# Attention without GpSimd, a planned tail of expert products, and six weight tiles converted early, in a fused attention and two-expert kernel

## Chip, cores and metric

One core of a Trainium2 chip runs the whole program. The metric is the device time of one execution in microseconds. TensorE (PE) multiplies, VectorE (DVE), ScalarE (ACT) and GpSimd (POOL) do the elementwise work, SyncE (SP) issues most transfers.

## What is computed

```python
scores = scale * q @ k.T                      # 4 batches x 8 heads, 576 x 576, head size 64
thresh = scores.max(-1) - tau
attn = softmax(where(scores >= thresh, scores, -1e9))
x = (attn @ v) as [2304 tokens, 512]
h = x @ w_in; g = max(h,0) + alpha*min(h,0); x = g @ w_out      # 512 -> 2048 -> 512
h = x @ w_in2; out = (h * sigmoid(h)) @ w_out2                  # 512 -> 2048 -> 512
```

All is float32. The experts' products are made from three single-pass products of a high and a low part (TERMS), so weights and activations are split into a high and a low half first.

## The kernel before

**Attention.** The 32 heads are worked in 16 pairs. A pair has 9 units: units 0 to 7 are 128 query rows of one of the two heads, unit 8 holds the last 64 rows of both. For each unit PE makes the scores (L333, two units at a time, eight products of 288 columns; unit 8 four products), DVE copies them out of PSUM and takes the row extreme (L347, "max"), ACT takes the exponential (L360), a small ACT instruction makes the threshold (L367), and DVE masks and sums (L373, "mask": two inputs from SBUF). PE transposes the masked rows (L408), ACT copies the transposes out (L123), PE multiplies with v (L442, L449). The reciprocal of the row sums (L382, DVE) is spread over 64 columns (L388, POOL), transposed by PE (L414), copied by ACT, and multiplied in as DVE takes the result out of PSUM (L456, L463) into X. The scores have two PSUM tiles of two banks (psS), transposes three banks, results one.

**Order.** Nothing is scheduled by the compiler inside attention: each operation is entered in a table with engine, assumed duration, priority and what it needs, and `plan` writes out one order for each engine from these durations. PE's order is fixed by the list CYCLE (Q score products, T transposes of the masked rows, R the bank with the last key block, Tr the transposes of the spread reciprocals, P the products with v, each with the pair it belongs to); the other engines take what is ready, by priority. PE changes its kind of product (`mode`) 11 times in a cycle of one pair.

**Weights.** `wconv` (L149 to L173) turns one 128 x 512 weight tile, loaded as 64-bit numbers into `wraw`, into its two halves: three ACT instructions, four on DVE (L159, L161, L163, L173) and two on POOL (L169, L171). Four of the first group's eight tiles are converted within attention, from unit WI = 60 on, one every WS = 12 units; the input split of the first 512 tokens (`xs0`, L548) follows from unit 104 on.

**Experts.** A job is a group of 512 hidden columns by a chunk of 512 tokens (the last 256): four blocks of hidden columns of 12 products each (`mm_h`, L202) into one of four PSUM banks, the activation on ACT and DVE (L211, L212 or L221, L222), its split (L123, L119), and, three blocks later, the products of `ymm` (L590, L599). The input split of later chunks is ACT and POOL work (L123, L119). These instructions are placed by the compiler's scheduler, which also merges them between those of attention. Their pools lie in the memory that attention's pools leave, and wait for the whole of these. The last products are added to ACC2 on DVE (L609) and stored by SP (L610).

Of the kernel before, what the change touches and what calls it, by code (L numbers as in the profile page):

```python
# [33 lines left out]
WI = 60  # L34
WU = 9
WS = 12
WN = 4
# [3 lines left out]
WT = 30  # L41
# [10 lines left out]
def mode(n):  # L52
    return {"pv": "v", "pv8": "v", "t": "t", "tr": "t"}.get(n[0], "t" if n[1] % 9 == 0 else "q")


def plan(ops, order, seq):
# [14 lines left out]
    def able(e):  # L71
        return [n for n in cand[e] if e != "PE" or n == seq[pe]]

    while any(able(e) for e in free):
# [3 lines left out]
        if e == "PE":  # L78
            pe += 1
            if mode(n) != last:  # L80
                t = max(t, free[e] + SWITCH)
            last = mode(n)
# [13 lines left out]
def attn_moe_moe(  # L96
# [52 lines left out]
    def wconv(stage, pool, wi, wo, g, j):  # L149
# [26 lines left out]
    def load_w(stage, pools, wi, wo, g, r0=()):  # L176
        r = list(r0)
        for j in range(len(r), NC + G):
            it = wconv(stage, pools[j // NC], wi, wo, g, j)
# [18 lines left out]
    def mm_h(ps, w, fl, xs, n):  # L198
        k = 0
        for c in range(NC):  # L200
# [31 lines left out]
    wA, xs0 = [], {}  # L232

    with ExitStack() as pa:
# [9 lines left out]
        psS = ent(name="psS", bufs=2, space=PSUM)  # L244
# [32 lines left out]
        warm = psT.tile([128, 512], F32, tag="t", name="t")  # L277
        for _ in range(WU):
            T.matmul(warm, zero[:, :128], zero, start=True, stop=True)
# [16 lines left out]
        def load(i):  # L296
            src = q_in[pairs[i]], k_in[pairs[i]]
            after = [qk(9 * (i - 2) + 1)] if i > 1 else []
# [3 lines left out]
            for x in (1, 0):  # L302
                def go(x=x):
                    nc.sync.dma_start(raw(i)[:, x, :QW[x]], src[x])
                op(("ld", i, x), "SP", 0.0 if i == 0 else 0.6, 1 if i else -4, after, go if i else lambda: None, 3.9 - 0.6 * x if i == 0 else 3.6)
            loadv(i, after, 2)

        def first(src):
# [3 lines left out]
            nc.sync.dma_start(raw(0)[:, 0, 512:], src[0][:, 512:])  # L312
            A.dma_start(sc[:, 0:1], tau[0:1].unsqueeze(0).to_broadcast([128, 1]))
            nc.sync.dma_start(raw(0)[h0, 0, :512], src[0][h0, :512])
            A.dma_start(raw(0)[h1, 0, :512], src[0][h1, :512])
# [68 lines left out]
        def spread(i, ch):  # L384
# [3 lines left out]
            P.tensor_copy(RS[i, ch][:, :n], stat(i)[:, 2, a:z].unsqueeze(2).to_broadcast([128, n, 64]))  # L388
# [285 lines left out]
```

## Time and profile before

| | |
|---|---|
| median of 3 runs | 1095.7 us (1095.08 to 1095.94) |
| the profiled execution: time / span | 1095.02 us / 1093.2 us |
| PE busy | 1077.0 us (99%) |
| DVE / ACT / POOL busy | 745.0 / 599.1 / 413.6 us |
| mean granted TensorE clock | 0.994 |
| first score product / last product with v / first product after it | 4.66 / 305.71 / 308.27 us |

Attention takes the first 307 us, the experts the rest. Because busy PE hides slow products, the table is read with rows that show starts of instructions: the distance between the same instruction in two pairs is the time of a pair.

### The profile page before, as it was taken

The numbers are of one execution on the slowest core, as the hardware profiler recorded it, in microseconds if no ns is written. First come the engines' busy times: TensorE is split into PE (matmuls) and PEld (weight loads), VectorE is DVE, ScalarE is ACT, GpSimd is POOL, SyncE is SP. The second block draws the span as 40 slices with busy tenths as digits, with TensorE's granted clock in tenths as the row PEclk, the third lists the DMA queues.
The fourth block names the chain that finished last, engine by engine and source line by source line (L and its number), as shares of the span: only waits on it lengthen the run. The fifth ranks groups of instructions, "written<-read, shape, count | busy, mean of one in ns | idle before, by whom it ended". The sixth has DMA issues, their size and how long they took to land.

```text
span 1093.2 us, 15460 instructions
## 1 busy us (share of the span) xinstructions
PE 1077.0 (99%) x5705; PEld 837.9 (77%) x5705; DVE 745.0 (68%) x1382; ACT 599.1 (55%) x1129; POOL 413.6 (38%) x339
## 2 busy tenths in 40 slices
PE   8999999999999999999999999999999999999998
PEld 5666656556767888888888888888888888888887
DVE  6989999989456677848755883764378568634343
ACT  5777878877555765535533553564555445334321
POOL 0100131320155566528525662662365346424210
PEclk8999999999999999999999999999999999999999
DMA  3212222211022222201110120121012002000112
GB/s 105 65 60 65 79 84 85 79 60 41 19 78 77 77 62 75 77 1 58 63 34 20 60 77 1 39 78 39 1 58 78 20 20 78 1 1 1 39 58 77
DMA packets 19259, 57.10 MB, mean 52 GB/s; under 512 B 2416, under 2 KB 2544, under 8 KB 19184
## 3 DMA queue, kind: packets, MB, share of 16 engines
q1 hardware_dynamic: 18880, 55.84, 15.8%
q8 instruction: 45, 0.74, 0.3%
q10 hardware_dynamic: 304, 0.28, 0.1%
q14 instruction: 30, 0.25, 0.1%
HBM read 51.39 MB, written 4.72 MB: 51 GB/s over the span
## 4 chain that ended last, share of the span: by engine, by line
PE 74%; DVE 6%; issue 3%; POOL 2%; ACT 2%; DMA 0%; DVEq 0%; POOLq 0%; ACTq 0%; SPq 0%
PE h L202 33%; PE y L599 18%; PE y L590 14%; PE s L333 3%; PE pv L442 3%; PE t L408 3%; DVE e L373 2%; POOL we L171 1%; DVE x L347 1%; DVE wa L161 1%; POOL wa L169 1%; DVE w L173 0%; ACT acc L228 0%; DVE wm L159 0%; DVE r L212 0%
## 5 line engine op out<-in xcount | busy, mean ns | idle before, releaser
L202 PE MATMUL h<-xs,w 128*128 128x512 f32 (+1 forms) x1920 | 431.1, 368 | 3.1 <-DVE r L212 3.1
L202 PEld LDWEIGHTS h<-xs,w 128*128 128x128 f32 x1920 | 337.8, 188 | 66.2 <-DVE r L212 4.9
L590 PE MATMUL y<-g,w 128*128 128x512 f32 (+1 forms) x960 | 215.0, 368 | 0.4 <-ACT acc L228 0.4
L599 PE MATMUL y<-w,g 128*128 128x512 f32 x864 | 213.7, 390 | 0.0
L590 PEld LDWEIGHTS y<-g,w 128*128 128x128 f32 x960 | 169.0, 188 | 31.6 <-ACT acc L228 0.7
L599 PEld LDWEIGHTS y<-w,g 128*128 128x128 f32 x864 | 160.7, 188 | 32.4
L119 DVE TENSOR_TENSOR g<-r,g 128x512 fp32r<-128x512 f32 (+1 forms) x160 | 140.7, 879 | 52.4 <-ACT g L123 51.1
L169 POOL TENSOR_TENSOR wa<-wa,w 128x512 f32<-128x512 f32 x64 | 84.0, 1313 | 207.3 <-ACT w L165 86.2
L119 POOL TENSOR_TENSOR xs<-acc,xs 128x512 fp32r<-128x512 f32 (+1 forms) x80 | 106.5, 1361 | 133.2 <-ACT xs L123 133.1
L123 ACT ACTIVATE g<-r 128x512 fp32r<-128x512 f32 (+1 forms) x160 | 94.0, 588 | 90.0 <-DVE r L222 46.6
L119 POOL TENSOR_TENSOR xs<-X,xs 128x512 fp32r<-128x512 f32 (+1 forms) x76 | 104.2, 1399 | 57.5 <-ACT xs L123 57.3
L347 DVE TENSOR_SCALAR_CACHE_REDUCE x<-s,nsc 128x576 f32<-128x576 f32 x144 | 112.4, 815 | 13.0 <-PE s L333 11.5
L360 ACT ACTIVATE e<-x,m 128x576 f32<-128x576 f32 x128 | 96.3, 781 | 43.5 <-DVE x L347 42.9
L373 DVE SCALAR_TENSOR_TENSOR e<-x,m,e 128x577 f32<-128x577 f32 x128 | 110.1, 881 | 8.1 <-ACT m L367 7.7
L222 DVE TENSOR_TENSOR r<-h,r 128x512 f32<-128x512 f32 (+1 forms) x80 | 50.7, 634 | 95.0 <-ACT r L221 94.9
L333 PE MATMUL s<-raw 64*128 64x288 f32 (+1 forms) x576 | 110.3, 437 | 5.1 <-DVE x L347 4.3
L388 POOL COPY rb<-m 128x256 f32<-128x256 f32 (+1 forms) x48 | 27.6, 576 | 211.8 <-PE t L414 100.3
L173 DVE TENSOR_TENSOR w<-we,wa 128x512 fp32r<-128x512 f32 x64 | 58.7, 918 | 61.1 <-POOL we L171 52.0
L221 ACT ACTIVATE r<-h 128x512 f32<-128x512 f32 (+1 forms) x80 | 43.8, 548 | 102.5 <-PE h L202 102.0
L171 POOL TENSOR_TENSOR we<-we,wm 128x512 f32<-128x512 f32 x64 | 93.6, 1462 | 13.7 <-ACT wm L167 13.1
L212 DVE SCALAR_TENSOR_TENSOR r<-r,neg,h 128x512 f32<-128x512 f32 (+1 forms) x80 | 55.0, 689 | 48.6 <-ACT r L211 48.4
L165 ACT ACTIVATE w<-wa 128x512 fp32r<-128x512 f32 x64 | 40.5, 633 | 82.2 <-DVE wa L161 75.4
(63 smaller groups left out, 1054.9 us busy)
## 6 DMA issues: line engine op xcount, KB each, us to landing
wraw<-in_w1i SPq DMA_DIRECT2D x16, 512.0 KB, 3.7
wraw<-in_w1o SPq DMA_DIRECT2D x16, 512.0 KB, 3.4
wraw<-in_w2i SPq DMA_DIRECT2D x16, 512.0 KB, 3.6
wraw<-in_w2o SPq DMA_DIRECT2D x16, 512.0 KB, 3.5
rv<-in_v SPq DMA_DIRECT2D x16, 480.0 KB, 3.4
raw<-in_q SPq DMA_DIRECT2D x15, 320.0 KB, 3.2
out<-o SPq DMA_DIRECT2D x18, 256.0 KB, 2.0
raw<-in_k SPq DMA_DIRECT2D x15, 288.0 KB, 2.8
```

The lines of the kernel that those rows point to most:

```text
L119: le.tensor_tensor(out=lo, in0=src, in1=hi.bitcast(F32), op=ALU.subtract)
L123: e.activation(out=dst, in_=src, func=AF.Copy)
L169: nc.gpsimd.tensor_tensor(out=a, in0=a, in1=w[:, 0].bitcast(F32), op=ALU.subtract)
L171: nc.gpsimd.tensor_tensor(out=e, in0=e, in1=m, op=ALU.mult)
L173: V.tensor_tensor(out=w[:, 1], in0=e, in1=a, op=ALU.add)
L202: nc.tensor.matmul(ps[:, :n], w[c][:, a, fl * 128:(fl + 1) * 128], xs[c][:, b, :n], start=k == 0, stop=k == 3 * NC - 1,)
L333: T.matmul(SP[u + k][:, hf, :S // 2], RAW[i][p, 0, q], RAW[i][p, 1, c], start=True, stop=True)
L347: V.tensor_scalar(out=x.rearrange("p (a b) -> p a b", a=2), in0=SP[u][:, :, :S // 2], scalar1=nsc, scalar2=None, op0=ALU.mult, op1=ALU.min ...
L360: A.activation(out=ES[u], in_=xts[u % XB][:, 1:S + 1], func=AF.Exp, bias=mcol(u, 0), scale=-1.0)
L373: V.scalar_tensor_tensor(out=e, in0=x, scalar=mcol(u, 1), in1=e, op0=ALU.is_le, op1=ALU.mult, accum_out=mcol(u, 2))
L590: nc.tensor.matmul(ys[e][:, :n], w[NC + fl][:, a, e * 128:(e + 1) * 128], gt[:, c, :n], start=fl == 0 and k == 0, stop=fl == G - 1 and k == 2,
L599: nc.tensor.matmul(ys[s], gt[:, a, s * 128:(s + 1) * 128], w[NC + fl][:, c, :], start=fl == 0 and k == 0, stop=fl == G - 1 and k == 2,)
```

## The change

- POOL leaves attention: the spread becomes an ACT instruction, and the two POOL instructions of `wconv` go to DVE there (the experts' later weights keep POOL).
- Six weight tiles instead of four are converted from unit 20 on, one every 14 units; the other two of the first group begin near the end of attention (unit 140). The split of the second chunk of tokens is also made in attention's table, on ACT and DVE.
- The units are worked as 0 to 8 instead of 8, 0 to 7, the CYCLE is another, with 9 changes of mode. The first pair's loads are cut otherwise, and the next pair's loads wait for the first score product.
- PE's order may take in fillers where `plan` sees PE idle: 32 products of zeros (z) at the start, and the 16 pieces (three products each) of the first job's hidden products (h), which now go into the two score tiles at the end of attention.
- The experts' pools wait tile by tile (`reuse_waits="tile"`); their four hidden banks are opened when the score tiles are given back.
- The last output tile is multiplied, added and stored in two column halves, the second stored by ACT's queue.

```diff
-WI = 60
+WI = 20
+WT = 4
-WS = 12
-WN = 4
+WF = 32
+WS = 14
+WN = 6
-    "T0:-1 T4:-1 Tr0:-1 Rr0:-1 Tr8:0 Rr8:0 Q4:0 Tr1:-1 P0:-1 "
-    "P8:0 Q6:0 P1:-1 P2:-1 Rr1:-1 T1:0 Q8:1 T2:0 T3:0 "
-    "T5:0 Q0:1 P3:-1 P4:-1 T6:0 T7:0 Q2:1 T8:1"
+    "Q2:-1 T6:-2 T2:-2 T7:-2 T0:-2 Tr1:-2 Q4:-1 T8:-2 Rr1:-2 "
+    "P0:-2 P1:-2 P2:-2 Q6:-1 T3:-1 T4:-1 T1:-1 Q8:-1 Tr8:-2 "
+    "T5:-1 Tr0:-1 Rr8:-2 Rr0:-1 Q0:0 P3:-2 P8:-2 P4:-2"
...
-        return [n for n in cand[e] if e != "PE" or n == seq[pe]]
+        c = cand[e]
+        if e == "PE":
+            fill = [n for n in c if n[0] in "hz"]
+            c = [n for n in c if n == seq[pe]]
+            if fill and (not c or ready[c[0]] > max(free[e], ready[fill[0]]) + ops[fill[0]][1]):
+                c = fill
+        return c
...
-        nc.gpsimd.tensor_tensor(out=a, in0=a, in1=w[:, 0].bitcast(F32), op=ALU.subtract)
-        nc.gpsimd.tensor_tensor(out=e, in0=e, in1=m, op=ALU.mult)
+        e2.tensor_tensor(out=a, in0=a, in1=w[:, 0].bitcast(F32), op=ALU.subtract)
+        e2.tensor_tensor(out=e, in0=e, in1=m, op=ALU.mult)
...
-        seq = [(i, t) for i in range(NP) for t in (8, 0, 1, 2, 3, 4, 5, 6, 7)]
+        seq = [(i, t) for i in range(NP) for t in range(9)]
...
-            P.tensor_copy(RS[i, ch][:, :n], stat(i)[:, 2, a:z].unsqueeze(2).to_broadcast([128, n, 64]))
+            A.activation(out=RS[i, ch][:, :n], in_=stat(i)[:, 2, a:z].unsqueeze(2).to_broadcast([128, n, 64]), func=AF.Copy)
...
-        for j in range(WN):
-            conv(j, [qk(WI + j * WS if j < NC else NU - WT)])
+        for j in range(NC + G):
+            conv(j, [qk(WI + j * WS if j < WN else NU - WT)])
...
+                need = [("h", f, c - 1)] if c else [("h", f - 1, NC - 1), ("max", NU - 2 + f // 2)]
+                op(("h", f, c), "PE", 0.68, 0, need + [("xl", 0, c), ("w", c, 9)], go, 0.9)
...
+        for k in range(WF):
+            op(("z", k), "PE", 0.22, 0, [("z", k - 1), ("ld8",)], idle)
...
-        ent = lambda **k: pb.enter_context(tc.tile_pool(**k))
+        ent = lambda **k: pb.enter_context(tc.tile_pool(reuse_waits="tile", **k))
...
+                    parts = 2 if g == NG - 1 and ti == NT // 128 - 1 else 1
+                    wd = DM // parts
...
+                            q = nc.scalar if x else nc.sync
+                            q.dma_start(out[ti * 128:(ti + 1) * 128, cs], o[:, cs])
```

## Rows read from the trace of the kernel before

**Rows 1.** The page, busy time, share of the span and instructions of PE.

```profile
PE 1077.0 (99%) x5705; PEld 837.9 (77%) x5705; DVE 745.0 (68%) x1382; ACT 599.1 (55%) x1129; POOL 413.6 (38%) x339
```

**Rows 2.** Windows: busy time (instructions) by engine, granted clock, DMA share, GB/s.

```profile
10.00:25.00 15.00, 15.00 (x81) 10.51 (x80) 12.59 (x37) 9.26 (x20) 1.33 (x3) 0.66 0.13 42
...
225.00:230.00 5.00, 5.00 (x34) 2.14 (x32) 4.41 (x11) 3.89 (x8) 0.00 (x0) 0.66 0.00 0
...
125.00:240.00 115.00, 109.79 (x750) 65.07 (x747) 109.25 (x282) 91.98 (x180) 29.19 (x30) 0.99 0.23 73
```

**Rows 3.** Timeline of PE, unit 8's scores of four pairs: start, duration, [idle before].

```profile
20.84 1.40 PE L333 MATMUL s<-raw 128*128 128x288 f32 x4
...
87.69 1.14 PE L333 MATMUL s<-raw 128*128 128x288 f32 x4
...
121.74 1.14 PE L333 MATMUL s<-raw 128*128 128x288 f32 x4
...
250.76 1.14 PE L333 MATMUL s<-raw 128*128 128x288 f32 x4
```

**Rows 4.** Timeline of PE from 36.3 to 40.5 us.

```profile
36.34 0.60 PE L408 MATMUL t<-ident,e 128*128 128x128 f32 x4
36.77 1.14 PE L333 MATMUL s<-raw 128*128 128x288 f32 x4
37.75 1.47 PE L408 MATMUL t<-ident,e 128*128 128x128 f32 x12
39.15 1.42 PE L333 MATMUL s<-raw 64*128 64x288 f32 x8
```

**Rows 5.** Timeline of DVE, POOL and PE: two maxes; a mask beside GpSimd.

```profile
119.68 0.82 DVE L347 TENSOR_SCALAR_CACHE_REDUCE x<-s,nsc 128x576 f32<-128x576 f32 x1
...
120.42 0.81 DVE L347 TENSOR_SCALAR_CACHE_REDUCE x<-s,nsc 128x576 f32<-128x576 f32 x1
...
139.28 1.78 POOL L171 TENSOR_TENSOR we<-we,wm 128x512 f32<-128x512 f32 x1
...
139.86 1.82 DVE L373 SCALAR_TENSOR_TENSOR e<-x,m,e 128x577 f32<-128x577 f32 x1
...
142.48 1.23 PE L333 MATMUL s<-raw 64*128 64x288 f32 x6 [0.59 <-DVE x L347]
```

**Rows 6.** Timeline of POOL, DVE and PE from 217 to 227 us.

```profile
217.40 5.88 POOL L119 TENSOR_TENSOR xs<-X,xs 128x512 fp32r<-128x512 f32 x4 [4.44 <-ACT xs L123]
...
222.09 1.81 DVE L373 SCALAR_TENSOR_TENSOR e<-x,m,e 128x577 f32<-128x577 f32 x1
...
224.70 2.34 PE L333 MATMUL s<-raw 64*128 64x288 f32 x8 [0.27 <-DVE x L347]
```

**Rows 7.** Timeline of DVE and PE, the first 12 us.

```profile
5.63 0.15 DVE L137 TENSOR_SCALAR ge<-sc 128x1 f32<-128x1 f32 x1 [4.22 <-DMA sc<-in_tau]
...
6.60 1.63 PE L333 MATMUL s<-raw 64*128 64x288 f32 x8 [0.80 <-DMA raw<-in_q]
...
9.59 2.27 PE L333 MATMUL s<-raw 64*128 64x288 f32 x8 [1.36 <-DVE x L347]
```

**Rows 8.** Timeline of ACT and PE after attention, and PE's waits in total.

```profile
306.84 1.09 ACT L211 ACTIVATE r<-h 128x512 f32<-128x512 f32 x2 [1.33 <-PE pv L442]
...
308.27 3.92 PE L202 MATMUL h<-xs,w 128*128 128x512 f32 x16 [1.53 <-DVE r L212]
...
PE h L202 <- DVE r L212: 3.1, 3, 1.5
```

**Rows 9.** Timeline of DVE: instructions of the conversion and of the input split.

```profile
125.06 0.41 DVE L159 TENSOR_SCALAR wm<-wm 128x512 int32<-128x512 int32 x1
...
225.31 1.88 DVE L548 TENSOR_TENSOR xs<-X,xs 128x512 fp32r<-128x512 f32 x3
```

**Rows 10.** Lines by form: ACT's smallest copy out of PSUM (count, busy us, mean ns).

```profile
L123 ACT ACTIVATE q<-t 128x256 f32<-128x256 f32 x16 | 6.3, 394 | 0.0
```

**Rows 11.** Timeline of DVE at the end of the program.

```profile
1088.89 1.29 DVE L609 TENSOR_TENSOR o<-y,X 128x512 f32<-128x512 f32 x2 [3.14 <-PE y L599]
```

More of the change, by code (lines that the diff above doesn't have):

```diff
@@ L196, in xsplit, with mm_h @@
         return xs
-    def mm_h(ps, w, fl, xs, n):
-        k = 0
-        for c in range(NC):
+    def mm_h(ps, w, fl, xs, n, cs=range(NC)):
+        k = 3 * cs[0]
+        for c in cs:
             for a, b in TERMS:
@@ L230, in accum @@
             V.tensor_tensor(out=dst, in0=ps, in1=dst, op=ALU.add)
-    wA, xs0 = [], {}
+    scores = ctx.enter_context(ExitStack())
+    psS = scores.enter_context(tc.tile_pool(name="psS", bufs=2, space=PSUM, side="right"))
+    wA, xs0, hs0 = [], [{}, {}], {}
     with ExitStack() as pa:
@@ L276, in attn_moe_moe, with idle @@
         ops = {}
-        warm = psT.tile([128, 512], F32, tag="t", name="t")
+        warm = psV.tile([128, 512], F32, tag="pv", name="pv")
+        def idle():
+            T.matmul(warm, zero[:, :128], zero, start=True, stop=True)
         for _ in range(WU):
-            T.matmul(warm, zero[:, :128], zero, start=True, stop=True)
+            idle()
         def op(name, eng, dur, prio, deps, fn, fin=None):
@@ L504, in attn_moe_moe @@
                 free = users(etiles[n][0], 2 * etiles[n][1]) if n >= 0 else []
-            op(("exp", u), "ACT", 0.667, 0, [("max", u)] + free, lambda u=u: expo(u), 0.82)
+            op(("exp", u), "ACT", 0.667, 2, [("max", u)] + free, lambda u=u: expo(u), 0.82)
             g = 0 if t == 8 else t // 2 + 1
@@ L513, in attn_moe_moe @@
                 op(("recip", i, ch), "DVE", 0.1, 0, us, lambda i=i, ch=ch: recip(i, ch), 0.25)
-                op(("spread", i, ch), "POOL", 0.4, 0, [("recip", i, ch), ("tr", bank.get(before.get((i, ch))))], lambda i=i, ch=ch: spread(i, ch), 0.6)
+                op(("spread", i, ch), "ACT", 0.18 if ch == 2 else 0.28, 1, [("recip", i, ch), ("tr", bank.get(before.get((i, ch))))], lambda i=i, ch=ch: spread(i, ch), 0.34 if ch == 2 else 0.44)
         order = {}
@@ L537, in attn_moe_moe @@
                 order["pv", i, kt] = ("pv", i, kt - 1)
[L538 to L548 removed]
+            op(("evac", i), "DVE", 0.62, -1, [("pv", i, KT - 1)], lambda i=i: evac(i), 0.78)
@@ new lines, in attn_moe_moe, with go @@
+        for f in range(G):
+            for c in range(NC):
+                def go(f=f, c=c):
+                    if f % 2 == 0 and c == 0:
+                        hs0[f] = psS.tile([128, 2, 512], F32, tag="s", name="s")
+                    mm_h(hs0[f - f % 2][:, f % 2], wA, f, [xs0[0][x] for x in range(NC)], 512, (c,))
+                need = [("h", f, c - 1)] if c else [("h", f - 1, NC - 1), ("max", NU - 2 + f // 2)]
+                op(("h", f, c), "PE", 0.68, 0, need + [("xl", 0, c), ("w", c, 9)], go, 0.9)
+                order["h", f, c] = need[0]
@@ L616, in attn_moe_moe @@
             oi = order.index((m, g))
-            if xs0:
-                xs = [xs0.pop(c) for c in range(NC)]
+            if (m, g) == (1, 0) and t0 < 1024:
+                xs = [xs0[t0 // 512][c] for c in range(NC)]
             else:
@@ L622, in attn_moe_moe @@
             for fl in range(G):
-                ps = psH.tile([128, 512], F32, tag="h", name="h")
-                mm_h(ps, w, fl, xs, n)
+                if (m, g, t0) == (1, 0, 0):
+                    ps = hs0[fl - fl % 2][:, fl % 2]
+                else:
+                    if psH is None:
+                        scores.close()
+                        psH = ent(name="psH", bufs=4, space=PSUM, side="right")
+                    ps = psH.tile([128, 512], F32, tag="h", name="h")
+                    mm_h(ps, w, fl, xs, n)
                 gt = (act1 if m == 1 else act2)(bt, bg, ps, g * G + fl, n, 512, nc.scalar, V)
```

91 lines of the change are left out of this document (48 added, 43 removed).

## The prediction

> **What bounds the kernel now.** I read the page first. PE is busy 99% of the span [rows 1], but a PE that waits inside a product or runs at half clock is busy too, so I looked at the distance between equal instructions. Unit 8's score products start at 87.69 and, two pairs later, at 121.74 [rows 3]: 17.02 us a pair. Is that PE's own work? Twelve transposes that start at 37.75 are followed at 39.15 by the next scores, and four that start at 36.34 by unit 8's at 36.77 [rows 4]: 0.108 for one transpose, no idle time between, and about 0.10 more where the kind of product changes (1.40 less 12 x 0.108). So in an undisturbed pair PE is the bound, with DVE close behind: two maxes start 0.74 apart [rows 5], and 18 of these and of the equally long masks make 13.3 us of the 17.
>
> Then I looked for pairs that take longer. From 121.74 to 250.76 lie seven pairs and 129.0 us [rows 3]; seven undisturbed ones take 119.2, so 9.8 us are lost there, in the stretch in which weights are converted. Rows 5 show the commonest kind: POOL's product for a weight runs from 139.28 for 1.78, the mask beside it takes 1.82 instead of 0.82, and the scores behind it wait until 142.48. The lost time is the mask's extra 1.0. The stretch has three of these, 3.0 us. The other 6.8 fall in one place: four POOL subtractions of a later chunk's split, merged into attention by the compiler, hold POOL for 5.88 from 217.40, a mask again takes 1.81, PE runs dry [rows 6], and the windows show a granted clock of 0.66 for 225 to 230, that is, part of it at 1.2 GHz instead of 2.4 [rows 2]. Eight products that start at 224.70 take 2.34.
>
> The start is the second place: unit 8's first scores are at 4.66 and the next pair's at 20.84 [rows 3], 16.2 us in which PE has only some 8 us of work at full clock (four pairs of scores at 1.35 by rows 4, unit 8 at 0.98, the rest about 1.6, my estimate). The granted clock for 10 to 25 is 0.66 and DVE is busy 12.59 of the 15 us [rows 2].
>
> The third is the border: after attention PE waits 1.53 for DVE and in all 3.1 us at three places [rows 8], the later two with the weights that were not converted in time, and 0.4 for an ACT copy. From there on, PE runs 785 us of expert products without gaps, and nothing in the change makes them fewer.
>
> **The change, part by part.**
>
> *Fewer changes of kind.* 9 instead of 11 a pair, 2 x 0.10 x 16 pairs: about -3.0. This counts in full only while PE is the bound.
>
> *POOL out of attention.* The collisions go, up to -9.8. What takes their place is DVE work. A weight tile cost DVE four instructions and now six: four with two inputs at 0.63 (1.88 for three, the end shared) and two at 0.41 [rows 9], 3.3 us. One tile every 14 units is 2.15 a pair, with 13.3 for maxes and masks and some 1.3 for outputs and reciprocals (estimate): 16.75 of a pair's 16.83. So DVE has hardly any slack from unit 20 to unit 104. These instructions come last by priority, and a late weight hurts nobody until unit 144, so they slide; but one that has begun holds back a max for up to 0.63, PE waits for the max, and two score tiles give little cover. Lower end: nothing is lost, since in the before too a pair with conversion work but no collision shows no loss. Upper end: each of 36 instructions holds PE for 0.3 on average, 11 us. I take 1.5, near the lower end, because the rows nearest to it (conversion work in undisturbed pairs) cost nothing: net -8.3.
>
> A rule of the Trainium skill speaks against this part: "VectorE: DVE Perf Modes", section "The DRAIN you can't avoid", says that an instruction cannot issue until the one before has emptied the pipe, and to keep the count of instructions low. In rows 5 the second max starts 0.74 after the first, which lasts 0.82: the trace has the two overlap. By the rule DVE would need more than PE in these pairs; its time stands with the rivals.
>
> *The spread on ACT.* POOL's work becomes three ACT instructions a pair of at most 256 columns. The nearest row is a copy of 256 out of PSUM, 0.39 [rows 10]; 3 x 0.39 is 1.2 a pair. ACT is busy 92 of 115 us in the conversion stretch [rows 2], 80%, and goes to 87%. It hides behind PE, if the queue is kept: the spread stands between exponentials, and behind it wait PE's Tr transposes and then P's last block. If that cover goes, a late Tr costs at most one exponential, about 0.7, a pair. I take zero, since the list puts Tr several products after the masks.
>
> *The start.* The fillers keep PE occupied where it waited 0.80 for q and 1.36 for a max [rows 7], and the next pair's loads no longer compete with the first q. The first max still waits for tau, which lands at 5.6 in both [rows 7]. DVE then needs 15 instructions of 0.74, 11.1 us, until about 21; it took 15. So at most 3.9 is to be had; at worst the fillers (32 x 0.22, 7 us) are in PE's way by about 1. I take -2.5, because half the stretch ran at half clock and the score products at 2.3 and more sit in the chain from score to max. What is late next is the masks.
>
> *The end of attention.* The first job's 48 hidden products already lie between the last pairs' products (the scheduler did it), so moving them into the list gains about nothing. Converted weights and the second chunk's split take away two of three waits, about 2.0 [rows 8]. The first wait I expect to stay: ACT's activation starts at 306.84, released by the last product with v [rows 8], because its tile lies in memory that attention's last tiles hold; waiting tile by tile helps only where the tile under it is free earlier. Here a hidden bank lies in a two-bank score tile, so the next job waits for two activations instead of one, up to +0.7. Together -1.7, with -3.5 and +0.7 as ends. DVE gets two tiles (6.6) and eight splits (5.0) here; in the tail there are hardly any maxes left, so it hides.
>
> *Transfers.* SP issues the weight loads earlier and waits at each for its one staging buffer; behind it stand the loads of the pair after next, needed more than a pair later, so nothing. Attention's ACT queue takes the same small number of loads at the start.
>
> *The last tile.* Two additions, 1.29 in all, end the kernel [rows 11]; with halves there are three, serial on DVE, the last one shorter, its store half the size. I take 0, with 0.3 either way.
>
> **Sum.** 3.0 + 8.3 + 2.5 + 1.7 = 15.5 off the profiled execution's 1095.0, so 1079.5. The profiled one stands 0.7 below the median of 1095.7; for the median I give 1080.
>
> **Rivals.**
>
> *DVE at its limit.* Conversion instructions hold maxes back by 0.3 each, without PE running dry: 11 instead of 1.5, so 1089.5. For it: 16.75 of 16.83. Against it: undisturbed conversion pairs at 17.02 before. 0.12.
>
> *Merged work comes back.* The change does not do what it says: with pools that wait tile by tile the compiler can place later splits or weights, POOL's among them, into attention's end, and the event of rows 6 happens once again there, 6.8: 1087. Against it: the second chunk's split is in the table now, and the third needs buffers that only the first job's products free. 0.10.
>
> *DVE starves PE (slower).* Where DVE falls behind for longer than PE's list can bridge, PE runs dry and its clock falls to 1.2 GHz as after 224. Each time costs the 6.8 of that place. With all six tiles, 41 us: about 1120. It decides from three such events on (15.5 / 6.8). For it: no slack on DVE. Against it: that event needed ACT, POOL and DVE late together. 0.05.
>
> *DVE issues at full durations.* 18 x 0.82, 1.6 for the rest and 2.3 for the conversion, with no overlap, make 18.7 a pair against 16.83, over nine pairs 17 us: 1097, no change within the error. That is what the skill's DRAIN section named above would give; rows 5 speak against it. 0.03.
>
> *More than I count.* The masks beside POOL's small copies get shorter too, the pair falls to 16.5 and the start and border give their upper ends: 1080 - 5 - 1.4 - 1.8, about 1072. 0.08.
>
> **Numbers.** The forecast has 0.62, its own range 1076 to 1084. For 8 in 10 the range must reach the first two rivals on one side and part of the last on the other: 1072.5 to 1090. A difference of 0.2%, 2.2 us, is what a measurement of this kernel can tell from none. Faster: forecast, first two rivals and the last, 0.92; same 0.03; slower 0.05.
>
> **What the new profile would show.** Right: 16.8 a pair for most pairs, no mask above 0.9 until the last pair, a granted clock of 1.00 for 10 to 25 and 225 to 230, POOL idle until the experts, the second pair's scores earlier by two or three us, no wait of the hidden products for weights. Wrong: PE's scores waiting for DVE in many pairs between units 20 and 104 (the limit), a POOL subtraction before the last product with v beside a long mask (merged work), a clock below 1.00 after 30 us (starving), or fillers that run while a max is ready.

## The result and the profile after

The changed kernel takes 1078.1 us (median of four runs, 1078.02 to 1078.86) against 1095.6 for the kernel before on the same chip: a ratio of 0.9842, interval [0.9825, 0.9859]. 1080.0 was forecast, 1072.5 to 1090. The profiled execution took 1078.86, its span 1077.1, so 16.1 of span are gone. The total fits; its parts do not, as the rest of this document shows.

The page of the changed kernel: busy time, share of the span and instructions of each engine.

```profile
PE 1067.9 (99%) x5749; PEld 835.3 (78%) x5749; DVE 745.3 (69%) x1403; ACT 606.3 (56%) x1177; POOL 357.4 (33%) x271
```

Beside [rows 1], POOL has lost 56 us of work and, but for short instructions in the first 6 us, is idle until 287 us; PE's 99% says as little as before. The windows of the changed kernel (columns as in [rows 2]):

```profile
10.00:25.00 15.00, 14.77 (x85) 8.50 (x84) 13.62 (x39) 10.62 (x21) 0.00 (x0) 1.00 0.16 45
125.00:240.00 115.00, 114.36 (x841) 70.99 (x840) 114.14 (x317) 101.14 (x214) 0.00 (x0) 1.00 0.26 79
225.00:230.00 5.00, 5.00 (x31) 2.58 (x29) 5.00 (x13) 5.00 (x11) 0.00 (x0) 1.00 0.03 10
295.00:305.00 10.00, 7.35 (x26) 5.56 (x25) 7.23 (x11) 4.63 (x8) 5.29 (x4) 0.83 0.17 52
```

The clock is full (2.4 GHz) where it was 0.66, at 10 to 25 and 225 to 230. DVE is busy 114.14 of 115 us in the conversion stretch, up from 109.25. And there is a new low clock, 0.83, at 295 to 305, which is the border (the passage from attention to the experts).

Now the pairs. The timeline of PE of the changed kernel: unit 8's scores of five pairs and, behind the first, the scores that follow; ahead of these the first scores of the third pair, and at the end those of the last:

```profile
36.28 1.24 PE L345 MATMUL s<-raw 64*128 64x288 f32 x8
...
99.81 1.14 PE L345 MATMUL s<-raw 128*128 128x288 f32 x4
...
101.97 1.24 PE L345 MATMUL s<-raw 64*128 64x288 f32 x8
103.14 1.08 PE L454 MATMUL pv<-pt,rv 128*64 128x512 f32 x4
...
132.62 1.14 PE L345 MATMUL s<-raw 128*128 128x288 f32 x4
...
198.24 1.14 PE L345 MATMUL s<-raw 128*128 128x288 f32 x4
...
216.35 1.14 PE L345 MATMUL s<-raw 128*128 128x288 f32 x4
...
249.37 1.14 PE L345 MATMUL s<-raw 128*128 128x288 f32 x4
...
251.53 1.24 PE L345 MATMUL s<-raw 64*128 64x288 f32 x8
```

A pair is now 16.41 us (99.81 to 132.62 are two), where it was 17.02 and 16.8 was forecast. From 132.62 to 249.37 seven pairs take 116.75; seven times 16.41 is 114.9, so 1.9 are lost instead of 9.8. Nearly all of that is one pair, 18.11 from 198.24.

**Where the 16.1 us are.** The last product with v starts at 305.71 in the kernel before and at 278.57 now, 27.1 earlier. In the kernel before, the 48 hidden products of the first job lay ahead of it in five groups, which took 11.6 by the distance of each to what follows it (285.19 to 289.41, 292.65 to 294.82, 295.61 to 296.85, 297.21 to 299.81, 300.39 to 301.71). Now they follow it in one row and take 11.0 (279.53 to 290.55). So attention itself is 15.6 shorter, and the hidden products 0.5. The last pair's first scores are, in the kernel before:

```profile
267.81 1.14 PE L333 MATMUL s<-raw 128*128 128x288 f32 x4
```

With it the 15.6 can be divided. The third pair begins at 36.28 instead of 36.77 [rows 4], so start and first two pairs gave 0.5. The last pair begins 16.3 earlier (251.53), so the 13 pairs between gave 15.8: 13 by 0.61 are 7.9, and the long pairs are the other 7.9 (9.8 - 1.9). The last pair and the tail behind it, without the hidden products, take 0.7 longer. From the last product with v to the last additions (1088.89 [rows 11] and 1072.73 now), the hidden products left out on both sides, lie 783.2 and 783.1: the border and all that follows gave nothing. The end after them is unchanged.

**A pair, from inside.** Why 0.61 a pair where two changes of kind at 0.10 were counted? The timeline of PE of the kernel before, the scores behind unit 8's of [rows 3]; under it a window of 0.02 us (90.30 to 90.32) of the same scores, and last such a window (102.05 to 102.07) of the changed kernel's:

```profile
90.07 1.57 PE L333 MATMUL s<-raw 64*128 64x288 f32 x8
91.57 1.08 PE L442 MATMUL pv<-pt,rv 128*64 128x512 f32 x4
...
90.07 0.51 PE L333 MATMUL s<-raw 64*128 64x288 f32 x1
...
101.97 0.51 PE L345 MATMUL s<-raw 64*128 64x288 f32 x2
```

And DVE's timeline in the kernel before, a mask and the readout that ends a max:

```profile
87.92 0.94 DVE L373 SCALAR_TENSOR_TENSOR e<-x,m,e 128x577 f32<-128x577 f32 x1
...
90.27 0.08 DVE L347 DVE_READ_ACCUMULATOR x<-s,nsc 128x1 f32 x1
```

The eight products are two units of four, one on each half of the array's rows, and run side by side: at 101.97 in the new kernel both start together (x2) and the group passes in 1.17 (to 103.14). At 90.07 in the kernel before one of them runs alone (x1 at 90.30); the other needs the score tile that the max gives back at 90.35, and the group takes 1.50 (to 91.57). That is 0.33, once a pair, and no view of idle time shows it, because PE is busy. What is left of the 0.61 is 0.28: the two changes of kind, 0.14 each by this subtraction.

The 0.33 may have two causes. The old list puts these scores close behind the max. But the mask at 87.92 also runs beside one of POOL's spread copies and takes 0.94 where its neighbours take 0.79 to 0.81, and DVE has no gap from there to that max. So up to 0.13 of the 0.33 can be POOL's copy, which the change took out as well; the runs below do not separate the two.

**The long pair.** The timeline of DVE, then of PE, of the changed kernel:

```profile
201.33 0.69 DVE L180 TENSOR_TENSOR w<-we,wa 128x512 fp32r<-128x512 f32 x1
201.94 0.68 DVE L565 TENSOR_TENSOR xs<-X,xs 128x512 fp32r<-128x512 f32 x1
202.54 0.81 DVE L359 TENSOR_SCALAR_CACHE_REDUCE x<-s,nsc 128x576 f32<-128x576 f32 x1
203.27 0.82 DVE L359 TENSOR_SCALAR_CACHE_REDUCE x<-s,nsc 128x576 f32<-128x576 f32 x1
...
209.12 1.23 PE L345 MATMUL s<-raw 64*128 64x288 f32 x6 [0.64 <-DVE x L359]
```

One product of the conversion and one of the split, back to back, put 1.21 us ahead of two maxes; another such two (198.65 and 199.25) lie 2.7 us before. DVE has no free time to make that up, and some units later scores wait. No long instruction and no low clock is involved; this is what is left of 9.8.

**The start.** PE, then DVE, of the changed kernel:

```profile
5.14 1.88 PE L345 MATMUL s<-raw 64*128 64x288 f32 x8
...
20.43 1.35 PE L345 MATMUL s<-raw 64*128 64x288 f32 x8
...
7.05 0.82 DVE L359 TENSOR_SCALAR_CACHE_REDUCE x<-s,nsc 128x576 f32<-128x576 f32 x1 [1.28 <-PE s L345]
```

The first scores are now two units' eight products instead of unit 8's four. They take 1.88 here, at a full clock, and the first max starts at 7.05, where it started at 6.11. The order of units alone does not explain that: in the ten runs below that begin with the same scores, they take 1.24 to 1.97 and the first max starts at 6.36 to 7.14. What stretches them was not found. The fillers keep the clock up, and from the first max to the second pair's first scores pass 13.4 us now (7.05 to 20.43) and 14.7 before (6.11 to 20.84 [rows 3]), where 11.1 were counted: between the maxes DVE still waits for the threshold that ACT makes (0.36, 0.37 and 0.27) and for unit 8's scores (0.59). So the second pair starts 0.4 earlier here, where 2.5 were forecast; in the nine other runs with the fillers its scores start at 19.53 to 20.49.

**The border.** PE, DVE, ACT and POOL of the changed kernel, after attention:

```profile
279.53 11.18 PE L209 MATMUL s<-xs,w 128*128 128x512 f32 x48
...
298.80 4.51 PE L625 MATMUL y<-g,w 128*128 128x512 f32 x12 [2.65 <-ACT g L130]
...
292.07 1.78 DVE L126 TENSOR_TENSOR g<-r,g 128x512 fp32r<-128x512 f32 x1
293.77 1.50 DVE L166 TENSOR_SCALAR wm<-wm 128x512 int32<-128x512 int32 x1
295.31 1.66 DVE L168 SCALAR_TENSOR_TENSOR wa<-wraw,wm 128x512 int32<-128x512 int32 x1
...
297.00 0.63 ACT L172 ACTIVATE w<-wa 128x512 fp32r<-128x512 f32 x1 [3.88 <-DVE wa L168]
...
290.30 6.12 POOL L126 TENSOR_TENSOR xs<-X,xs 128x512 fp32r<-128x512 f32 x4
```

The hidden products no longer wait for anything: the three waits of [rows 8], 3.1, are gone. In their place y waits once, 2.65, for the third hidden tile's ACT copy. Read the queues backwards: that copy stands in ACT's queue behind L172, which rounds a weight tile of the second group and waits 3.88 for DVE; DVE's instructions for it (L166, L168) take 1.50 and 1.66 instead of 0.43 and 0.68, as POOL does the subtractions of the third chunk's split beside them. The clock falls behind the wait: the next 12 products take 4.31 (the hidden products after them start at 303.11) where 12 take 2.72 at full clock (36 from 290.64 to 298.80 in a run below). 0.83 over 10 us is 3.4 us at 1.2 GHz, 1.7 lost. Three waits have turned into one, with other work ahead of it.

**The end.** The last additions of the changed kernel:

```profile
1072.73 1.35 DVE L646 TENSOR_TENSOR o<-y,X 128x512 f32<-128x512 f32 x3 [3.30 <-PE y L641]
```

Three additions take 1.35 where two took 1.29 [rows 11]. From there to the end of the span are 4.4 us, and 4.3 before.

### The profile page after: what moved, and what is told of

Read it like the earlier page. It is cut to its first block, busy times and chain, and to the rows that moved or that the text cites. A ratio compares the mean times of both kernels' runs of the same rounds, so it can differ in the third digit from the quotient of the medians.

```text
span 1077.1 us, 15422 instructions
## 1 busy us (share of the span) xinstructions
PE 1067.9 (99%) x5749; PEld 835.3 (78%) x5749; DVE 745.3 (69%) x1403; ACT 606.3 (56%) x1177; POOL 357.4 (33%) x271
## 4 chain that ended last, share of the span: by engine, by line
PE 94%; DVE 3%; ACT 1%; issue 1%; DMA 0%; POOL 0%; DVEq 0%; ACTq 0%; SPq 0%
PE h L209 36%; PE y L641 18%; PE y L625 18%; PE s L345 8%; PE t L420 6%; PE pv L454 6%; DVE x L359 1%; PE pv L288 1%; DVE e L385 1%; PE t L461 1%; PE t L426 1%; DMA wraw<-in_w1i 0%; ACT pt L130 0%; DVE wa L168 0%; DVE wm L166 0%
## 5 line engine op out<-in xcount | busy, mean ns | idle before, releaser
L209 PE MATMUL h<-xs,w 128*128 128x512 f32 (+1 forms) x1872 | 418.7, 368 | 0.0
L209 PEld LDWEIGHTS h<-xs,w 128*128 128x128 f32 x1872 | 329.8, 189 | 60.1
L176 POOL TENSOR_TENSOR wa<-wa,w 128x512 f32<-128x512 f32 x56 | 72.9, 1302 | 458.8 <-ACT w L172 359.9
L126 DVE TENSOR_TENSOR g<-r,g 128x512 fp32r<-128x512 f32 (+1 forms) x160 | 140.0, 875 | 56.3 <-ACT g L130 54.9
L126 POOL TENSOR_TENSOR xs<-acc,xs 128x512 fp32r<-128x512 f32 (+1 forms) x80 | 106.0, 1355 | 133.5 <-ACT xs L130 133.4
L126 POOL TENSOR_TENSOR xs<-X,xs 128x512 fp32r<-128x512 f32 (+1 forms) x72 | 98.7, 1399 | 57.5 <-ACT xs L130 57.1
L219 DVE SCALAR_TENSOR_TENSOR r<-r,neg,h 128x512 f32<-128x512 f32 (+1 forms) x76 | 52.2, 686 | 73.8 <-ACT r L218 73.6
L345 PE MATMUL s<-raw 64*128 64x288 f32 (+1 forms) x576 | 100.6, 429 | 0.9 <-DVE x L359 0.9
L385 DVE SCALAR_TENSOR_TENSOR e<-x,m,e 128x577 f32<-128x577 f32 x128 | 99.7, 811 | 1.2 <-ACT m L379 1.0
L345 PEld LDWEIGHTS s<-raw 64*128 64x128 f32 (+1 forms) x576 | 57.2, 188 | 40.8 <-DVE e L385 11.4
L172 ACT ACTIVATE w<-wa 128x512 fp32r<-128x512 f32 x64 | 40.7, 635 | 84.4 <-DVE wa L168 77.5
L178 POOL TENSOR_TENSOR we<-we,wm 128x512 f32<-128x512 f32 x56 | 81.6, 1457 | 18.2 <-ACT wm L174 18.2
```

The lines of the kernel that those rows point to most:

```text
L126: le.tensor_tensor(out=lo, in0=src, in1=hi.bitcast(F32), op=ALU.subtract)
L176: e2.tensor_tensor(out=a, in0=a, in1=w[:, 0].bitcast(F32), op=ALU.subtract)
L178: e2.tensor_tensor(out=e, in0=e, in1=m, op=ALU.mult)
L209: nc.tensor.matmul(ps[:, :n], w[c][:, a, fl * 128:(fl + 1) * 128], xs[c][:, b, :n], start=k == 0, stop=k == 3 * NC - 1,)
L345: T.matmul(SP[u + k][:, hf, :S // 2], RAW[i][p, 0, q], RAW[i][p, 1, c], start=True, stop=True)
L385: V.scalar_tensor_tensor(out=e, in0=x, scalar=mcol(u, 1), in1=e, op0=ALU.is_le, op1=ALU.mult, accum_out=mcol(u, 2))
```

## The experiments

The first four start from the changed kernel and undo one part each. A ratio is to the kernel before on the same chip, and its medians there are 1094.8 to 1095.6; so a difference of 1 us between two runs says little.

**The conversion's last two products back on GpSimd.**

```diff
-            it = wconv(stage, (wpa, wpo)[j // NC], w1i, w1o, 0, j, V)
+            it = wconv(stage, (wpa, wpo)[j // NC], w1i, w1o, 0, j, P)
...
-        WOPS = [("SP", 0.6)] + [("ACT", 0.52), ("DVE", 0.34), ("DVE", 0.61), ("DVE", 0.34), ("ACT", 0.52), ("ACT", 0.52), ("DVE", 0.61), ("DVE", 0.61), ("DVE", 0.61)]
+        WOPS = [("SP", 0.6)] + [("ACT", 0.52), ("DVE", 0.34), ("DVE", 0.61), ("DVE", 0.34), ("ACT", 0.52), ("ACT", 0.52), ("POOL", 1.23), ("POOL", 1.23), ("DVE", 0.61)]
```

> The changed kernel, but within attention the two last products of a weight tile's conversion go back to GpSimd (1.3 to 1.8 us each in the table's order). Theory: a mask that meets such a product takes 1.8 instead of 0.8 us and PE's scores wait for it; with six tiles that is 4 to 8 us more than the changed kernel, about 1083 to 1086, and the masks of 1.8 us are in the trace beside the pairs that are 1 us longer. Rival: DVE is the tight engine, and taking 1.2 us per tile from it helps: the same or up to 2 us faster.

Measured: 1081.65 (1081.04 to 1082.66), ratio 0.9883 [0.9868, 0.9898], 3.6 more than the changed kernel and a little less than expected. The timelines of POOL, DVE and PE of this run:

```profile
112.07 1.28 POOL L176 TENSOR_TENSOR wa<-wa,w 128x512 f32<-128x512 f32 x1 [18.76 <-ACT w L172]
...
112.12 1.85 DVE L385 SCALAR_TENSOR_TENSOR e<-x,m,e 128x577 f32<-128x577 f32 x1
...
118.00 1.24 PE L345 MATMUL s<-raw 128*128 128x288 f32 x4 [1.10 <-DVE x L359]
```

The long masks are back, six of 1.58 to 1.88 beside two-input POOL products (and a few of 1.2 to 1.3), with the waits of the scores behind them; pairs of 18.0 to 18.2 appear, and the last product with v is 4.1 later. DVE, with less to do (111.63 of 115 us), is no help. The collision is the cost, not DVE's sum of work, and the rival of a DVE at its limit falls.

**The spread back on GpSimd.**

```diff
-            A.activation(out=RS[i, ch][:, :n], in_=stat(i)[:, 2, a:z].unsqueeze(2).to_broadcast([128, n, 64]), func=AF.Copy)
+            P.tensor_copy(RS[i, ch][:, :n], stat(i)[:, 2, a:z].unsqueeze(2).to_broadcast([128, n, 64]))
```

and its entry in the list of operations from ACT to POOL, 0.4.

> The changed kernel, but the spread of the reciprocals goes back to GpSimd. The pair fell from 17.02 to 16.42 us, 0.4 more than the two saved changes of kind explain. Theory: GpSimd's copy stretched the mask beside it (0.94 instead of 0.82) and with it the max for which PE's next scores waited; then the pair goes back to 16.7 to 16.8, 4 to 6 us more in all. Rival: the other order of the products did it, and the pair stays at 16.4, within 1 us of the changed kernel.

Measured: 1076.09 (1075.58 to 1076.48), ratio 0.9832 [0.9816, 0.9849], 2.0 less than the changed kernel, though the two ratios' intervals overlap. A pair stays at 16.40 to 16.45, so PE's new list is enough to make the pair short. What the copies cost in the old list this run does not show: here only one mask is longer than 0.83 (0.94 at 23.28), where the kernel before has one of 0.92 to 0.95 in nearly every pair. The long pair of 18.1 becomes 16.86, and later ones take 16.65 to 16.87: most of the same loss, spread out. The border's wait is 2.3 instead of 2.65, and the clock stays at 1.00 there (290 to 305); part of the 2.0 comes from that, and part from the start, which is 0.9 shorter in this execution (unit 8's first scores at 17.52 instead of 18.41) and varies as much between other runs.

**No zero products at the start.**

```diff
-WF = 32
+WF = 0
```

> The changed kernel without the 32 products of zeros at the start. Theory of the prediction: with PE idle between the first scores its granted clock falls to 1.2 GHz as it did from 11 to 21 us before, and the first pairs take 2.5 us longer, about 1080.5. Rival: DVE and not PE sets the start, since the first max comes later than before and DVE runs nearly without gaps; then 0 to 1 us.

Measured: 1081.86 (1081.48 to 1082.10), ratio 0.9884 [0.9869, 0.9898], 3.8 more than the changed kernel; in the trace attention ends 2.2 later. A window of this run:

```profile
10.00:25.00 15.00, 12.61 (x56) 8.51 (x56) 12.28 (x35) 10.32 (x21) 0.00 (x0) 0.77 0.15 51
```

Without fillers the clock falls as it did before the change, 0.77 against 0.66 [rows 2]. By the trace they are worth about what the forecast gave the start. What the forecast missed is that the new order of units without them gains nothing: the second pair's scores start at 21.08 in this run, at 20.84 in the kernel before.

**Pools that wait as a whole; weights one job later.** Two edits that should act on the border:

```diff
-        ent = lambda **k: pb.enter_context(tc.tile_pool(reuse_waits="tile", **k))
+        ent = lambda **k: pb.enter_context(tc.tile_pool(**k))
```

> The changed kernel, with the experts' pools waiting for the whole of attention's pools again. Theory: waiting tile by tile lets the next group's weights into the queues of ACT, DVE and GpSimd while the first job's activation is due (PE waits 2.65 us and then runs 3.4 us at half clock); with whole-pool waits the activation of the first job starts later but weights do not stand ahead of it: within 2 us of the changed kernel, either way. Rival: the early start is worth what it was made for, and the kernel is 3 to 6 us slower.

```diff
-            if oi + 1 < len(order) and t0 == CH[0][0] or (m == 1 and g == 0):
+            if oi + 1 < len(order) and t0 == CH[1 if oi == 0 else 0][0]:
```

> The changed kernel, with the second group's weights loaded one job of 512 tokens later. Theory: at the border ACT stood 2.4 us waiting for a weight transfer ahead of the first activation, and conversions and splits stretched the rest, so that PE waited 2.65 us and ran 3.4 us at half clock; with the weights out of the way 3 to 4.5 us go, about 1074.5. Rival: the split of the third chunk on GpSimd beside DVE is enough to make the activations late, and less than 1.5 us go; or the later weights bring the wait back one job later.

Measured: 1077.95 (1077.28 to 1078.50), ratio 0.9848 [0.9833, 0.9863], and 1077.70 (1077.58 to 1078.43), ratio 0.9842 [0.9825, 0.9858]. Both kernels came out with the changed kernel's order of instructions on every engine. So the first shows only that the way of waiting does not matter here. The second says nothing on the border: moving the lines in the program did not move the loads. Another handle was needed, the next one.

**The second group's first weights held back.** A copy of one element from the first job's last hidden tile into the buffer makes each of the first two loads wait:

```diff
+        if hold is not None:
+            V.tensor_copy(raw[:1, 0, :1].bitcast(F32), hold[:1, 1, :1].bitcast(F32))
...
-            it = wconv(stage, pools[j // NC], wi, wo, g, j, nc.gpsimd)
+            it = wconv(stage, pools[j // NC], wi, wo, g, j, nc.gpsimd, hold if j < 2 else None)
...
-                getw(*order[oi + 1])
+                getw(*order[oi + 1], gt if oi == 0 else None)
```

> The changed kernel, with the second group's weight loads held until the first job's last activation is split (a one-element copy from that tile into the load's target stands before the first two loads). Theory: at the border these conversions, not the pools' waits, make PE wait 2.7 us and run 3.4 us at half clock; without them in the way 3 to 4.5 us go, about 1074. Rival: GpSimd's split of the third chunk slows DVE enough by itself, or the later weights are missed later: less than 1.5 us.

Measured: 1074.33 (1073.99 to 1074.62), ratio 0.9813 [0.9799, 0.9828], 3.8 less than the changed kernel. PE and DVE of this run at the border:

```profile
290.64 8.32 PE L627 MATMUL y<-g,w 128*128 128x512 f32 x36
298.80 8.32 PE L211 MATMUL h<-xs,w 128*128 128x512 f32 x36
...
296.40 0.20 DVE L159 COPY wraw<-g 1x1 f32<-1x1 f32 x2
```

The wait is gone and the clock is 1.00 from 290 to 305. The intervals of the two ratios just touch, but the trace shows the place: attention ends at 279.62 here and at 279.53 in the changed kernel, the last additions start at 1068.22 and 1072.73. POOL's split still slows L126 (1.37 at 289.99 instead of 0.69), which is harmless by itself. So the weights' instructions in ACT's and DVE's queues were the border's loss, some 4 us with the clock.

**Both: weights held back, spread on GpSimd.** The two edits above together.

> The same hold, and the spread of the reciprocals on GpSimd as in the second experiment, which was 1.6 us faster than the changed kernel. If the two gains are separate places (border, and the pair near 200 us with its late ACT), they add: about 1072.5. If the second experiment's gain was only that its border kept the full clock, nothing is added: as with the hold alone.

Measured: 1073.43 (1072.45 to 1073.58), ratio 0.9803 [0.9789, 0.9818], 0.9 less than with the weights held back alone. The intervals overlap: whether the spread belongs on ACT or on GpSimd is worth at most about 1 us here, and is not settled.

**The kernel before, with its spread on ACT.** The first of the two kernels that do one part alone: the second run's edit the other way round.

> The kernel before, with one part of the change alone: the spread of the reciprocals as an ACT instruction. Theory that GpSimd's copy holds up the mask and PE: the undisturbed pair falls from 17.02 to about 16.7, 4 to 5 us off, about 1091. Rival, that the order of the products makes the shorter pair: 17.0 as before, within 1 us of 1095.6.

Measured: 1107.73 (1106.62 to 1109.09), ratio 1.0117 [1.0102, 1.0132]: 12.5 slower, a case that neither expectation had. Its waits of PE in total (us, times, longest):

```profile
PE t L449 <- ACT q L123: 13.5, 9, 1.6
```

And the timelines of ACT and PE, one such place:

```profile
49.03 0.42 ACT L388 ACTIVATE rb<-m 128x256 f32<-128x256 f32 x1
...
49.81 1.45 ACT L360 ACTIVATE e<-x,m 128x576 f32<-128x576 f32 x2
51.33 0.39 ACT L123 ACTIVATE q<-t 128x256 f32<-128x256 f32 x1
...
51.76 0.69 PE L449 MATMUL t<-p,rv 128*64 128x64 f32 x16 [1.57 <-ACT q L123]
```

0.42 for the spread is what was counted. But in the old list P8's last block follows closely on the copies q and px, and ACT, in order, has the spread, px and two exponentials ahead of q; in the kernel before, q stands ahead of the exponentials there (48.69). Work that was cheap on an engine with 20% free time cost 12.5 through its place in the queue. In the new list P8 stands near the end, after Q0 and P3, and the spread costs at most about 1 us (the run above). Pairs without such a wait take 17.15 here and not less than 17.02. Their late scores are late by 0.16 instead of 0.33, as they would be without POOL's copy beside the mask, but ACT's new order moves DVE's instructions too, so this is no measure of the copy.

**The kernel before, with attention's conversion on DVE.** The first run's edit the other way round, in the kernel before.

> The kernel before, with one part of the change alone: the four conversions within attention wholly on DVE. Theory: the three masks of 1.8 us go and with them 3 us; the loss of 6.8 us at 210 to 230 us came from a later chunk's split on GpSimd and from ACT's copies for it, which stay, so 2 to 4 us off, about 1092.5. Rival, DVE at its limit: the added 1.2 us per tile hold back maxes, no gain or 1 to 3 us slower.

Measured: 1088.84 (1088.68 to 1089.23), ratio 0.9944 [0.9929, 0.9959], 6.4 less, more than expected. PE of this run:

```profile
121.24 1.14 PE L333 MATMUL s<-raw 128*128 128x288 f32 x4
...
243.81 1.14 PE L333 MATMUL s<-raw 128*128 128x288 f32 x4
```

The seven pairs of [rows 3] take 122.57, so 3.4 are lost (119.2 is their undisturbed time) instead of 9.8, though the merged split is still there (POOL is busy with it for 6.01 from 212.27). Its pair takes 20.12, 3.1 more, without a fall of the clock; in the kernel before, a weight's conversion on POOL lay in the same pair (211.17), and that pair took 23.95 (209.94 to 233.89), 6.9 more. So the losses do not simply add. The split also stands at another place of its pair here, and the runs do not separate that from the missing conversion.

**Two more changes of kind.** The changed kernel with one group of transposes moved between two products with v:

```diff
-    "T5:-1 Tr0:-1 Rr8:-2 Rr0:-1 Q0:0 P3:-2 P8:-2 P4:-2"
+    "Tr0:-1 Rr8:-2 Rr0:-1 Q0:0 P3:-2 T5:-1 P8:-2 P4:-2"
```

> The changed kernel with T5 moved in PE's list from behind Q8 to between P3 and P8: the same products, but 11 changes of kind a pair instead of 9. If the two saved changes are worth what the prediction gave them (0.10 each), the pair goes from 16.42 to 16.6 and the kernel to about 1080.7 (+3). If the shorter pair came from where the scores stand in the list and not from the changes of kind, the pair stays within 0.05 of 16.42.

Measured: 1085.51 (1085.36 to 1086.07), ratio 0.9917 [0.9901, 0.9934]: 7.4 more than the changed kernel and more than either expectation, though the border's wait is 2.2 here and the clock full. Pairs of 17.37 and 17.21 alternate (102.30 to 119.67, to 136.88): 17.29 on average, 0.88 more. PE of this run:

```profile
104.12 1.57 PE L345 MATMUL s<-raw 64*128 64x288 f32 x8
105.61 1.08 PE L454 MATMUL pv<-pt,rv 128*64 128x512 f32 x4
106.62 0.66 PE L420 MATMUL t<-ident,e 128*128 128x128 f32 x4
107.21 0.69 PE L461 MATMUL t<-p,rv 128*64 128x64 f32 x16
```

The two changes can be read directly. The products with v ahead of the moved transposes take 1.01 to the next group where such four take 0.91, the four transposes 0.59 where 4 x 0.11 are 0.44, and the products behind them 0.05 more: 0.30. The other 0.58 are groups that wait inside. The scores at 104.12 take 1.49 to the next group and, in every other pair, those at 112.18 take 1.42 (to 113.60), where 1.17 is free of waits, again one unit whose tile comes late; the rest are 0.1 to 0.2 in other groups. So a list does two things to a pair: it sets the changes of kind, at some 0.15, and it sets when scores meet their tiles.

**More work on DVE.** Each converted tile gets two more DVE products of 0.63 in attention, whose results are not used:

```diff
+        junk = qp.tile([128, 512], F32, tag="junk", name="junk")
+        def twice():
+            V.tensor_tensor(out=junk, in0=X[:, 0, :512], in1=X[:, 0, :512], op=ALU.mult)
...
+                for k in range(2 if s == 8 else 0):
+                    op(("wd", j, k), "DVE", 0.61, 9, prev, twice)
+                    prev = [("wd", j, k)]
```

> The changed kernel with two more DVE products of 0.63 us per converted tile, results unused (a measure of how much room DVE has). Six tiles within attention add 7.6 us of DVE. By the prediction's account DVE has 16.42 less 14.6 a pair free, about 25 us from unit 20 to the end, and needs 22; with 30 it would be over, and the masks or the late tiles cost 3 to 6 us. Rival: there is more room than counted because late weights only slide, 0 to 1.5 us.

Measured: 1087.55 (1087.01 to 1088.37), ratio 0.9935 [0.9920, 0.9950], 9.5 more than the changed kernel and more than either expectation. PE of this run:

```profile
302.06 9.61 PE L633 MATMUL y<-g,w 128*128 128x512 f32 x32 [10.74 <-ACT g L130]
```

Attention ends 0.6 later (280.14 against 279.53). The loss is at the border: a wait of 10.74 and a granted clock of 0.71 from 290 to 305. Low-priority work on a full DVE does slide, as the forecast said; but it slides to the border, where somebody does wait for it, and where it runs beside POOL's split: the last two extra products take 3.41 together (from 295.28) instead of some 1.3.

**Weights held back, and the first chunk's split spread out.** The weights held back as above, with the four pieces of the split started at four different units near the end instead of one:

```diff
-                src = [("evac", c), qk(NU - XO)] + ([("evac8", c), ("evac", HP + c), qk(NU - 1), ("xh", 0, c)] if ch else [])
+                src = [("evac", c), qk(NU - XO + 6 + 7 * c)] + ([("evac8", c), ("evac", HP + c), qk(NU - 1), ("xh", 0, c)] if ch else [])
```

> The ninth experiment (held weights, spread on ACT) with the four splits of the first 512 tokens begun at units 110, 117, 124 and 131 instead of all from unit 104. Theory: the one pair of 18.1 us, from 198 to 216 us, comes from these splits falling together with the last conversion ahead of a max; apart, that pair goes back to 16.5, 1.6 us off, about 1072.7. Rival: the pair is long because of the transfers' or the list's place there, and stays; then 1074.3.

Measured: 1073.07 (1072.44 to 1073.23), ratio 0.9800 [0.9787, 0.9814], the shortest median of all. PE of this run:

```profile
197.77 1.14 PE L347 MATMUL s<-raw 128*128 128x288 f32 x4
...
214.17 1.14 PE L347 MATMUL s<-raw 128*128 128x288 f32 x4
...
264.20 1.14 PE L347 MATMUL s<-raw 128*128 128x288 f32 x4
```

The pair that took 18.11 takes 16.40, so the split's pieces in that place made it long. But the three pairs behind it now take 16.79, 16.73 and 16.51: the four together take 66.43 instead of 67.58 (198.24 to 265.82 in the changed kernel), and 1.2 of the 1.9 are won back. Attention ends 1.7 earlier than with the weights held back alone, but 0.5 of that lies ahead of unit 8's first scores, where the edit does nothing. The time is 1.3 less, and the intervals overlap.

## Why the prediction was right, and where it was not

By the spans 16.1 us went and 15.5 were forecast, and that they lie so close is luck: one term gave 4.9 more than counted, and three gave 4.3 less (2.0 at the start, 1.9 at the end of attention, 0.4 in POOL's part).

- **POOL out of attention**, net -8.3 forecast, -7.9 measured. Right, mechanism included: no mask in attention is longer than 0.82, POOL is idle until 287 but for a few short instructions in the first 6 us, and putting the conversion back brings the long masks and 3.6 us back. DVE's price of 1.5 was 1.9, paid in one pair. The trace also shows who is slowed. Beside POOL's two-input instructions DVE's mask went from 0.82 to 1.85, L168 from 0.68 to 1.66 and L126 from 0.69 to 1.78, while the maxes, whose scores lie in PSUM, took 0.78 to 0.82 throughout, beside POOL too. The Trainium skill, "GPSIMD Engine Reference", section "1. Specifications", names a shared interface to SBUF, with contention for DVE instructions that have two SBUF inputs; the trace agrees and gives the size.
- **Fewer changes of kind**, -3.0 forecast, -7.9 measured (13 pairs of 0.61). The step that failed is the sentence "in an undisturbed pair PE is the bound". PE was without idle time, but in each pair one unit's scores started 0.33 late, inside a busy group, as their tile was not yet given back. [rows 4] held a sign of it: the scores at 39.15 pass in 1.35, and such a group passes in 1.17 when both units start together. The forecast took the 1.35 for the price of the work. The new list lets the two units start together; that is 4.3 in the 13 pairs, of which up to 1.7 may be due to POOL's copies being gone. The changes themselves were 0.14 each instead of 0.10, 3.6 in all. The run with two changes more shows both again, 0.58 of late groups and 0.30 of changes. The Trainium skill, "TensorEngine Tiling (Array Packing)", section "Key Properties", says that changing the tiling mode drains TensorE. That such a change costs time agrees with the trace, 0.14 to 0.15 here; the drain itself no run shows.
- **The spread on ACT**, 0 forecast. Right, within about 1 us, for the new list alone: with the old list it costs 12.5. The forecast's condition, "if the queue is kept", is what the two runs separate, and its price for a lost cover, one exponential or about 0.7 a pair, is near the 0.78 a pair measured (12.5 / 16). That nearness is luck: PE waited for q at nine places, 1.5 each, behind two exponentials. And it was not Tr that came late: it was P's last block, behind the copy q.
- **The start**, -2.5 forecast, -0.5 measured. The mechanism held (fillers, full clock from 10 to 25; without them 2.2 more by the trace). Two steps failed. "The first max still waits for tau, which lands at 5.6 in both": the max now waits for the scores, 1.28 behind tau's last instruction here and 0.24 to 1.26 in the other runs. And of the 3.9 "to be had" most is not to be had: with the clock full, DVE still takes 13.4 for what was counted as 11.1, because it waits for ACT's thresholds and unit 8's scores between the maxes. Between executions the start varies by about 1 us, so the 0.5 is of these two; no run reaches 2.5.
- **The end of attention**, -1.7 forecast, +0.2 measured: the last pair takes 0.7 longer without hidden products between its own, these take 0.5 less in one row, and the border gave 0.0. The two waits went as argued. The first wait went too, which was not expected: the 48 hidden products now fill that time. But the rival "merged work comes back" came true here, and not in attention's end where it was put. With the first group's weights done, the compiler merges the second group's weights and the third chunk's split into the first job, and PE waits 2.65 and then runs at half clock. Holding two loads back gave 3.8.
- **Transfers and the last tile**, 0 forecast. Right: the final additions lie within 0.1 us of the end as before.
- **The rivals.** *DVE at its limit* and *DVE starves PE* fall: DVE is busy 99% of the conversion stretch, and yet extra work costs attention 0.6. *DVE issues at full durations* falls too. The maxes at 202.54 and 203.27 are 0.73 apart with a duration of 0.81, and a pair takes 16.4 where no overlap would give 18.7. The section "The DRAIN you can't avoid" of the Trainium skill ("VectorE: DVE Perf Modes"), read as full durations in a row, does not fit these rows, and the measurement decides; the section itself adds that a next operation that is not held starts earlier, which the forecast left out. *More than I count* was half right: the pair did fall to 16.4, but at most 0.13 of the 0.61 can come from the masks beside POOL's small copies, and start and border did not give their upper ends.

Of the signs named ahead, the clock, the idle POOL, the masks and the hidden products without a wait came true. The pair of 16.8 and the second pair two or three us earlier did not. One sign of being wrong, a clock below 1.00 after 30 us, came true at the border, outside attention.

## What to carry to other kernels

An engine that is never idle can still be waiting: compare the duration of the same group of instructions over the trace, and where a group is longer than its best by a constant amount, look for a wait inside it. Work moved to an engine with time to spare is priced by what stands behind it in that engine's queue, and the same move can be free under one order and cost 12 us under another. When work finishes earlier, look at what the compiler brings forward into its place; one small data dependency that holds the next loads back was worth a fifth of the whole change.

## What the runs showed of the hardware

- A DVE instruction with a single input was slowed beside POOL too: L166 took 1.50 at 293.77 instead of 0.43, more in proportion than the two-input ones (1.66 instead of 0.68). It ran beside a POOL subtraction with two inputs; a POOL copy such as the spread lengthened a mask at most to 0.95 in the kernel before, and in the run with the spread on GpSimd only one, to 0.94.
- Waits of nearly the same length at the border went with a clock that fell in some runs (2.65 in the changed kernel, 0.83 from 295 to 305; 2.4 with later weights, 0.89 from 290 to 305) and with a full clock in others (2.3 with the spread on GpSimd, 2.2 with two more changes of kind). Part of the difference between such runs is this and not the edit: 1.7 us by the windows of the changed kernel.
